# One wire for accumulating transfers in the plan of the order, and a hold for each kind of output product

## The chip, the cores and the metric

The kernel runs on one core of a Trainium2 chip. The metric is the time of the device in microseconds, the median of several executions; less is better. TensorE (PE) multiplies matrices, ScalarE (ACT) and VectorE (DVE) work on elements, GpSimd (POOL) and SyncE (SP) here issue transfers (DMAs). Each engine works through its instructions in the order in which they were written, and waits on semaphores for what the others make.

## What is computed

An attention block over channels and two expert layers, on 6016 tokens of 256 channels, in float32:

```python
def _attn_ref(q, k, v, tau):                  # q, k, v: (1, 6016, 256)
    qn = q / (norm(q, axis=1) + 1e-6); kn = k / (norm(k, axis=1) + 1e-6)
    a = softmax(kn.transpose(0, 2, 1) @ qn / tau)       # 256 x 256
    return v @ a

def _moe_ref(x, w_gate, w_val, w_out, rms_g):  # d_ff = 1536
    xn = x / sqrt(mean(x * x) + 1e-6) * rms_g
    return (silu(xn @ w_gate) * (xn @ w_val)) @ w_out

def _moe2_ref(x, w_in, w_out):                 # d_ff = 2048
    h = x @ w_in
    return (h - tanh(h)) @ w_out

reference = _moe2_ref(_moe_ref(_attn_ref(q, k, v, tau), ...), ...)
```

## The kernel before

**Tiles and stages.** Tokens lie along the free axis, in pairs of blocks of 512; the first pair is short and is worked last, as two blocks of 448. Every float32 product is made of three matmuls in a rounded float32 format: a high and a low part of each operand, and three of the four combinations (`prod`). The attention comes first (up to about 66 us), then the first expert layer, pair by pair, and from about 614 us on the second, in six groups, one for each pair of blocks: `SECOND` is the order 1, 2, 3, 4, 5, 0.

**A unit.** Two by two blocks (of tokens and of hidden channels) are multiplied by a scheme with seven products instead of eight (`unit`). It works in four PSUM banks X, T, Y, Z: X takes A11 B11, T takes S1 T1; ScalarE copies X to Y and T to a tile m5; Y takes S2 T2; VectorE adds Y and m5 to Z; X takes A12 B21 (result c11), Y takes S3 T3 (c22 = Y + m5), Z takes S4 B22 (c12), Y takes A22 T4 (c21). These seven are the main products. For the second layer each result passes through tanh on ScalarE and a subtraction on VectorE. A group has 8 units.

**The output products.** Of the last four units each result is split into high and low parts (`finish_block`; ScalarE makes the high part, VectorE the low one) and multiplied into two of the four accumulators (`Accumulate.push`). For the first four units (`SEVEN2 = 4`) the output too is made with seven products, on sums of the results (`second_seven`, `Seven`): W11 on c11, S1 on c11 + c12, N3 on c12 + c22, M2 on c11 + c12 + c22, and later W12 on c21, S4 on c22, W22 on c11 + c12 + c22 + c21. The sums are made in place by transfers that accumulate, SBUF to SBUF, issued by POOL (`add_by_dma`, line 460): c11 += c12; then c12 += c22 and c11 += c22; then c11 += c21. The second add into c11 must wait until both parts of S1 have been read from it, N3 must wait for one add and M2 for two. After four units `Seven.turn` copies the four accumulators to tiles `part` and combines them by four more adds, each needing the one before; they are used when the group's output leaves. A group so has 20 adds of 256 KB (224 KB in the last group), 120 in all. The split forms live in a ring of four buffers `uh` and `ul` (in the trace uW, uS, uN, uM and uc); each of W11, S1, N3 and M2 of a unit takes the buffer that the same form of the unit before had, and its split waits until that product is done.

**The order.** Nothing is emitted in the order of the loops. `Graph.op` collects each instruction with its engine, an estimate of its cost and the instructions that it must follow. `Graph.run` then plays the engines forward in time and lets each take, of the instructions that are ready, the most urgent; `Graph.latest` goes back from the end and gives each a latest time; six passes of both are made, the one with the earliest planned end is kept, and its order is emitted. For ScalarE, VectorE and the DMA queues, urgency is that latest time. For TensorE it is a key: the main products have the amount of main product work issued before them (`g.main`), and an output product has `g.main` at its birth plus a hold: `LAG0`, `LAG1`, `LAG2` for plain ones (`Accumulate.product`), `LAG7` for the forms (`Seven.form`). The hold is a priority, not a wait: when no instruction with a smaller key is ready, TensorE takes the held one. Transfers of SP are planned on a wire that they share: 1000 ns after issue or behind the one before, then their size at 390 bytes per ns, then 900 ns. An accumulating transfer is planned to occupy POOL for 900 ns and to land 3500 ns after its start (`ADD_LAND`, in `run` line 229 and in `latest` line 286), whatever the one before does. Stores and loads of SP and adds of POOL don't meet in the plan. The waits that the hardware makes are those of the real dependences; the estimates decide only the order.

Of the kernel before, what the change touches and what calls it, by code (L numbers as in the profile page):

```python
# [39 lines left out]
PATIENT, HOLD, TOLERANCE = ("ACT", "DVE"), 900.0, 60.0  # L40
DMA_SETUP, DMA_RATE, DMA_TAIL, DMA_ISSUE = 1000, 390.0, 900, 450
DMA_SLACK = 2200
ADD_ISSUE, ADD_LAND = 900, 3500
STALL, STALL_COST = 40.0, 300.0


# [53 lines left out]
class View:  # L100
# [5 lines left out]
    @property  # L106
    def ap(self):
        return self.f(self.buf.t)
# [14 lines left out]
class Graph:  # L123
# [38 lines left out]
    def run(self):  # L162

        ops = self.ops
        for o in ops:
            o.left, o.ready = len(o.preds), 0.0
        free = dict(READY)
        known = {e: [] for e in free}
        avail = {e: [] for e in free}
        soon = {e: [] for e in free}  # L170
        wire = lag = moved = 0.0

        def rank(o):
            return (o.key if o.eng == "PE" else o.idx if o.late is None else o.late, o.idx)

        def now_known(o):
            if o.eng not in DMAS:
                o.ready += o.slack
            heappush(known[o.eng], (o.ready, o.idx))
            if o.eng not in DMAS:  # L180
                coming(o, o.ready, AHEAD)

        def coming(o, ready, depth):
            for s, data in o.succs:
                if s.left == 1 and s.eng not in DMAS:
                    t = ready + o.cost + self.gap(o, s, data)
                    if s.eng in PATIENT:
                        soon[s.eng].append((t, s.idx))
                    if depth > 1:
                        coming(s, t, depth - 1)  # L190

        for o in ops:
            if not o.left:
                now_known(o)
        order = []
        while len(order) < len(ops):
            best = None
            for e in free:
                if avail[e]:
                    t = free[e]  # L200
                elif known[e]:
                    t = max(free[e], known[e][0][0])
                else:
                    continue
                if best is None or t < best[0]:
                    best = t, e
            t, e = best
            while known[e] and known[e][0][0] <= t:
                o = ops[heappop(known[e])[1]]
                heappush(avail[e], (*rank(o), o))  # L210
            o = heappop(avail[e])[2]
            if e in PATIENT and o.late is not None:
                soon[e] = [x for x in soon[e] if x[0] > t and ops[x[1]].left]
                o = self.patient(o, t, known[e] + soon[e], avail[e], ops, lag)
                if not isinstance(o, Op):
                    free[e] = o
                    continue
            o.start = t
            if e == "PE" and o.late is not None:
                lag = t - o.late  # L220
            if e == "SP":
                free[e] = t + o.cost
                wire = max(t + DMA_SETUP, wire) + o.size / (
                    RAMP_RATE if moved < RAMP_BYTES else DMA_RATE)
                moved += o.size
                o.end = wire + DMA_TAIL + o.slack
            elif e == "POOL":
                free[e] = t + o.cost
                o.end = t + ADD_LAND
            else:  # L230
                stalled = e == "PE" and t > 10 * COLD and t > free[e] + STALL
                o.end = free[e] = t + o.cost * (2 if e == "PE" and t < COLD else 1) + (
                    STALL_COST if stalled else 0.0)
            order.append(o)
            for s, data in o.succs:
                s.left -= 1
                s.ready = max(s.ready, o.end + self.gap(o, s, data))
            for s, _ in o.succs:
                if not s.left:
                    now_known(s)  # L240
        return order
# [28 lines left out]
    def latest(self, order):  # L270

        idle, before, dense = 0.0, None, {}
        for o in order:
            if o.eng == "PE":
                if before is not None:
                    idle += max(0.0, o.start - before)
                dense[o], before = o.start - idle, o.end
        end = max(o.end for o in order) - idle
        for o in reversed(order):
            late = end  # L280
            for s, data in o.succs:
                late = min(late, s.late - self.gap(o, s, data) - (
                    s.slack if s.eng == "PE" else 0.0))
            o.late = late - (
                DMA_SETUP + o.size / DMA_RATE + DMA_TAIL + o.slack if o.eng == "SP" else
                ADD_LAND if o.eng == "POOL" else o.cost)
            if o.eng == "PE":
                o.late = min(o.late, dense[o])

# [27 lines left out]
BEHIND = 4  # L317
WARM = 6
MARGIN = 450.0
LAG0, LAG1, LAG2 = 4100.0, 10000.0, 6500.0  # L320
SWAP7 = False
SEVEN2, LAG7 = 4, 5000.0
SKEW = 2


# [1 line left out]
def attn_moe_kernel(  # L327
# [42 lines left out]
    g = Graph()  # L370
# [92 lines left out]
    def prod(out, w, x, n, start, key=None):  # L463

        (wh, wl), (xh, xl) = w, x

        def emit():
            o = ap(out)
            for i, (a, b) in enumerate(((wh, xh), (wl, xh), (wh, xl))):
                nc.tensor.matmul(  # L470
                    o, ap(a), ap(b), start=start and i == 0, stop=i == 2, skip_group_check=True)

        return g.op("PE", 3 * (n / 2.4 + 13.7), emit, [wh, wl, xh, xl], [out], key=key)
# [813 lines left out]
    class Seven(Accumulate):  # L1287
# [10 lines left out]

        def form(self, j, name, u, t, m):
            first = self.begins(t, m)  # L1300
            prod(self.at(t, m), self.forms[j][name], u, self.sizes[t], first, key=g.main + self.lag7)

        def turn(self):
            n = self.sizes[0]
# [153 lines left out]
    def second_seven(j, x, n, A, keep):  # L1458
# [7 lines left out]
        def out(c):  # L1466
            def f(src):
                t = T[c]
                activation(t, src, AF.Tanh, n)
                tt("sub", t, src, t, n)  # L1470
                if c == "c11":
                    form("W11", "c11", 0, 0)
                if c == "c12":
                    add_by_dma(T["c11"], T["c12"])
                    form("S1", "c11", 1, 0)
                if c == ("c22" if SWAP7 else "c12"):
                    add_by_dma(T["c12"], T["c22"])
                    add_by_dma(T["c11"], T["c22"])
                    form("N3", "c12", 0, 1)
                    form("M2", "c11", 1, 1)  # L1480
                if c == "c21":
                    add_by_dma(T["c11"], T["c21"])
            return f
# [273 lines left out]
```

## Time and profile before

| | |
|---|---|
| median of 3 executions | 1112.81 us (1112.71 to 1113.14) |
| the profiled execution | 1114.58 us, of which 1112.8 from the first to the last instruction |
| TensorE busy | 1099.9 us (99%), 4872 matmuls |
| VectorE, ScalarE busy | 909.7 us (82%), 734.0 us (66%) |
| POOL | 126 instructions, 120 of them adds |
| mean granted clock of TensorE | 0.998 of full |

Times in rows are microseconds from the first instruction unless marked ns. PE is TensorE's matmuls, PEld its weight loads, one for each matmul. A matmul's record is longer than the distance to the next one's start, since they overlap. A tile's name is that of the program without its numbers: `uM` is the high part of form M2, `ulM` the low one, `keepwraw`, `keepvh`, `keepvl`, `keepw12h` hold c11, c22 and c21 of one unit or another, `wc` is c12, `l20h` to `l27h` are the weights of units 0 to 7.

### The profile page before, as it was taken

The numbers are of one execution on the slowest core, as the hardware profiler recorded it, in microseconds if no ns is written. First come the engines' busy times: TensorE is split into PE (matmuls) and PEld (weight loads), VectorE is DVE, ScalarE is ACT, GpSimd is POOL, SyncE is SP. The second block draws the span as 40 slices with busy tenths as digits, with TensorE's granted clock in tenths as the row PEclk, the third lists the DMA queues.
The fourth block names the chain that finished last, engine by engine and source line by source line (L and its number), as shares of the span: only waits on it lengthen the run. The fifth ranks groups of instructions, "written<-read, shape, count | busy, mean of one in ns | idle before, by whom it ended". The sixth has DMA issues, their size and how long they took to land.

```text
span 1112.8 us, 14515 instructions
## 1 busy us (share of the span) xinstructions
PE 1099.9 (99%) x4872; PEld 904.5 (81%) x4872; DVE 909.7 (82%) x1590; ACT 734.0 (66%) x1298; POOL 105.6 (9%) x126
## 2 busy tenths in 40 slices
PE   9999999999999999999999999999999999999998
PEld 8888988888888888888888768778778778878887
DVE  7899897987887888788866878888788888887876
ACT  7675466566566656656656777577587687676674
POOL 0000000000000000000000131130131130230230
PEclk9999999999999999999999999999999999999999
DMA  9952121113212311322322563463463462451451
GB/s 358 380 195 93 58 72 52 45 50 130 68 38 76 90 54 53 114 86 69 127 76 76 131 112 68 93 106 67 95 105 67 99 109 54 102 97 29 105 88 46
DMA packets 61644, 109.44 MB, mean 98 GB/s; under 512 B 7552, under 2 KB 18688, under 8 KB 61568
## 3 DMA queue, kind: packets, MB, share of 16 engines
q1 hardware_dynamic: 43856, 77.32, 20.6%
q0 software_dynamic: 17280, 30.81, 16.2%
q8 instruction: 38, 0.62, 0.2%
q10 hardware_dynamic: 432, 0.38, 0.1%
q14 instruction: 38, 0.31, 0.1%
HBM read 54.79 MB, written 22.83 MB: 70 GB/s over the span
## 4 chain that ended last, share of the span: by engine, by line
PE 70%; issue 11%; DMA 10%; DVE 3%; POOL 3%; ACT 2%; SPq 0%; POOLq 0%; DVEq 0%; ACTq 0%
PE acc L470 27%; PE Yv L470 6%; PE Yg L470 5%; PE Xg L470 4%; PE Xv L470 4%; PE Yh L470 3%; PE S L478 3%; PE v L470 2%; PE g L470 2%; PE Xh L470 2%; PE Zg L470 2%; PE Zv L470 2%; PE Tg L470 2%; PE Tv L470 2%; DMA keepvl<-keepvl 2%
## 5 line engine op out<-in xcount | busy, mean ns | idle before, releaser
L428 ACT ACTIVATE uc<-tc 128x512 fp32r<-128x512 f32 x120 | 74.7, 630 | 93.1 <-DVE tc L443 52.7
L447 DVE TENSOR_TENSOR ulc<-tc,uc 128x512 fp32r<-128x512 f32 x120 | 81.1, 684 | 7.6 <-ACT uc L428 6.9
L460 POOL DMA_DIRECT2D keepwraw<-wc x6 | 5.3, 890 | 767.7 <-DVE ulW L447 767.7
L447 DVE TENSOR_TENSOR ulc<-wc,uc 128x512 fp32r<-128x512 f32 (+1 forms) x96 | 64.5, 678 | 15.0 <-PE acc L470 13.3
L428 ACT ACTIVATE uc<-wc 128x512 fp32r<-128x512 f32 (+1 forms) x96 | 59.8, 623 | 21.4 <-PE acc L470 18.2
L443 DVE TENSOR_TENSOR Zv<-Yv,m5v 128x512 f32<-128x512 f32 x30 | 21.0, 699 | 37.8 <-ACT tc L428 18.2
L478 PE MATMUL S<-q,k 128*128 128x256 f32 x188 | 42.3, 385 | 0.8 <-DMA k<-k_in 0.8
L443 DVE TENSOR_TENSOR Zh<-Yh,m5h 128x512 f32<-128x512 f32 (+1 forms) x48 | 32.9, 685 | 10.2 <-PE Yh L470 6.8
L478 PEld LDWEIGHTS S<-q,k 128*128 128x128 f32 x188 | 35.9, 193 | 5.9 <-DMA q<-q_in 1.1
L428 ACT ACTIVATE wc<-Zh 128x512 f32<-128x512 f32 (+1 forms) x48 | 28.1, 585 | 19.1 <-PE Zh L470 18.4
L443 DVE TENSOR_TENSOR acc<-acc,sq 128x512 f32<-128x512 f32 (+1 forms) x46 | 29.4, 678 | 8.0 <-ACT sq L428 7.3
L428 ACT ACTIVATE m5h<-Th 128x512 f32<-128x512 f32 (+1 forms) x48 | 28.0, 583 | 11.1 <-PE Th L470 11.1
L443 DVE TENSOR_TENSOR wc<-Zh,wc 128x512 f32<-128x512 f32 (+1 forms) x48 | 32.4, 675 | 0.7
L443 DVE TENSOR_TENSOR s<-Yh,m5h 128x512 f32<-128x512 f32 (+1 forms) x48 | 32.3, 673 | 0.7 <-PE Yh L470 0.6
L428 ACT ACTIVATE tc<-Zg 128x512 f32<-128x512 f32 x30 | 17.9, 597 | 22.0 <-PE Zg L470 22.0
L470 PE MATMUL Yh<-T2h,l2s 128*128 128x512 f32 (+1 forms) x96 | 29.7, 390 | 2.4 <-ACT Yh L428 2.4
L428 ACT ACTIVATE tc<-Xg 128x512 f32<-128x512 f32 x30 | 18.0, 599 | 20.9 <-PE Xg L470 20.8
L443 DVE TENSOR_TENSOR tc<-Yg,m5g 128x512 f32<-128x512 f32 x30 | 20.6, 686 | 13.3 <-PE Yg L470 13.3
L428 ACT ACTIVATE Yh<-Xh 128x512 f32<-128x512 f32 (+1 forms) x48 | 27.6, 575 | 5.7 <-DVE wc L443 4.2
L470 PE MATMUL acc<-ulc,w12h 128*128 128x512 f32 x80 | 31.2, 390 | 0.0
L470 PE MATMUL acc<-uc,w11h 128*128 128x512 f32 x80 | 31.2, 389 | 0.0
L470 PE MATMUL acc<-uc,w10h 128*128 128x512 f32 x80 | 31.1, 389 | 0.0
(1094 smaller groups left out, 3849.2 us busy)
## 6 DMA issues: line engine op xcount, KB each, us to landing
vraw<-vT_in SPq DMA_DIRECT2D x11, 512.0 KB, 4.5
y<-r SPq DMA_DIRECT2D x22, 256.0 KB, 2.2
part<-part POOLq DMA_DIRECT2D x20, 256.0 KB, 3.3
outT<-part SPq DMA_DIRECT2D x20, 256.0 KB, 2.2
q<-q_in SPq DMA_DIRECT2D x8, 512.0 KB, 8.4
k<-k_in SPq DMA_DIRECT2D x8, 512.0 KB, 8.4
raw<-w_in_in SPq DMA_DIRECT2D x8, 512.0 KB, 3.9
l<-y SPq DMA_DIRECT2D x16, 256.0 KB, 2.2
```

The costliest lines, as they stand in the source:

```text
L428: nc.scalar.activation(out=ap(out), in_=ap(in_), func=func, **{x: ap(a) for x, a in kw.items()})
L443: return dve(lambda: f(out=ap(out), in0=ap(a), in1=ap(b)), n, 2, [a, b], [out])
L447: lambda: nc.vector.tensor_sub(out=ap(out), in0=ap(in_), in1=f32(ap(hi))), n, 2,
L460: g.op("POOL", ADD_ISSUE, lambda: nc.gpsimd.dma_start(out=ap(out), in_=ap(in_), accum_op=ALU.add), [in_, out], [out])
L470: nc.tensor.matmul(o, ap(a), ap(b), start=start and i == 0, stop=i == 2, skip_group_check=True)
L478: lambda: nc.tensor.matmul(ap(out), ap(a), ap(b), start=start, stop=stop, **kw),
```

## The change

The planned landing of an accumulating transfer changes from 3500 ns after its start to a wire that all of them share: 1850 ns after the start or when the one before has left the wire, 1450 ns on the wire, and 600 ns more. Going back, a POOL step counts 1850 + 1450 + 600 = 3900 ns. The hold of plain output products of the second layer changes from 6500 to 7000 ns of main work, and the one hold of 5000 ns for the forms becomes one for each: W11 4000, S1 and N3 8000, M2 9000, W12, S4 and W22 5000. All instructions are the same; their order on each engine is planned anew.

```diff
-ADD_ISSUE, ADD_LAND = 900, 3500
+ADD_ISSUE, ADD_SETUP, ADD_TIME, ADD_SLACK = 900, 1850, 1450, 600
...
-        wire = lag = moved = 0.0
+        wire = lag = moved = adds = 0.0
...
             elif e == "POOL":
                 free[e] = t + o.cost
-                o.end = t + ADD_LAND
+                adds = max(t + ADD_SETUP, adds) + ADD_TIME
+                o.end = adds + ADD_SLACK
...
-                ADD_LAND if o.eng == "POOL" else o.cost)
+                ADD_SETUP + ADD_TIME + ADD_SLACK if o.eng == "POOL" else o.cost)
...
-LAG0, LAG1, LAG2 = 4100.0, 10000.0, 6500.0
+LAG0, LAG1, LAG2 = 4100.0, 10000.0, 7000.0
 SWAP7 = False
-SEVEN2, LAG7 = 4, 5000.0
+SEVEN2 = 4
+LAG7 = dict(W11=4000., S1=8000., N3=8000., M2=9000., W12=5000., S4=5000., W22=5000.)
...
         def form(self, j, name, u, t, m):
             first = self.begins(t, m)
-            prod(self.at(t, m), self.forms[j][name], u, self.sizes[t], first, key=g.main + self.lag7)
+            prod(self.at(t, m), self.forms[j][name], u, self.sizes[t], first,
+                 key=g.main + self.lag7[name])
```

## Rows read from the trace of the kernel before

**Rows 1.** Stages: stretch, us, busy us (count) by engine, clock, DMA share, GB/s.
```profile
190.00:614.57 424.57, 424.57 (x1866) 348.35 (x1865) 342.21 (x619) 261.18 (x461) 0.00 (x0) 1.00 0.24 78
614.57:694.23 79.66, 77.26 (x326) 59.77 (x324) 65.74 (x105) 58.40 (x105) 17.63 (x20) 1.00 0.50 102
694.23:775.77 81.54, 80.85 (x350) 64.70 (x348) 67.72 (x108) 58.43 (x103) 17.45 (x20) 1.00 0.46 91
775.77:859.85 84.08, 81.99 (x350) 66.00 (x348) 67.88 (x108) 58.62 (x103) 17.45 (x20) 0.98 0.44 88
859.85:941.15 81.30, 80.65 (x350) 64.75 (x348) 67.75 (x108) 58.42 (x103) 17.42 (x20) 1.00 0.46 89
941.15:1023.02 81.87, 81.47 (x349) 64.61 (x348) 67.36 (x108) 57.35 (x102) 17.48 (x20) 1.00 0.41 78
1023.02:1108.40 85.38, 84.89 (x403) 74.80 (x401) 63.93 (x109) 54.42 (x104) 17.48 (x20) 1.00 0.36 67
```

**Rows 2.** Chain that ended last: start, us, what and how many in a row.
```profile
673.99 2.04 PE acc L470 x9
...
1075.23 1.86 PE acc L470 x9
```

**Rows 3.** Order of time: start, us, engine and instruction [idle before, releaser].
```profile
637.83 0.73 PE L470 MATMUL acc<-uM,l2q 128*128 128x512 f32 x2 [0.50 <-ACT uM L428]
...
1071.87 0.47 PE L470 MATMUL Yh<-T3h,l25h 128*128 128x448 f32 x1 [0.38 <-DVE Zh L443]
```

**Rows 4.** Order of time, three adds at the end of a group's fourth unit.
```profile
656.99 0.87 POOL L460 DMA_DIRECT2D keepvl<-keepw12h  x1 [3.58 <-DVE ulM L447]
657.59 1.16 POOL L460 DMA_DIRECT2D wc<-keepw12l  x1
659.00 0.86 POOL L460 DMA_DIRECT2D keepw12h<-keepw12l  x1 [0.25 <-issue]
661.98 0.63 ACT L428 ACTIVATE uN<-wc 128x512 fp32r<-128x512 f32 x1 [0.91 <-DMA wc<-keepw12l]
663.37 0.63 ACT L428 ACTIVATE uM<-keepw12h 128x512 fp32r<-128x512 f32 x1 [0.23 <-DMA keepw12h<-keepw12l]
665.46 0.70 DVE L443 TENSOR_TENSOR Zh<-Yh,m5h 128x512 f32<-128x512 f32 x1
666.21 0.50 PE L470 MATMUL Yh<-T3h,l25h 128*128 128x512 f32 x1 [0.93 <-DVE Zh L443]
```

**Rows 5.** DMA table, 614.57 to 1108.40: queue's share of 16 engines; issues, us to landing.
```profile
q0 software_dynamic: 17280, 30.81, 36.6%
...
part<-part POOLq DMA_DIRECT2D x20, 256.0 KB, 3.3
```

**Rows 6.** SP's order, a chain piece, order of time and stages around 801 us.
```profile
793.31 3.57 SPq L454 DMA_DIRECT2D outT<-part  x4
...
796.32 5.68 DMA keepwraw<-keepwraw
...
802.03 0.63 ACT L428 ACTIVATE uM<-keepwraw 128x512 fp32r<-128x512 f32 x1 [1.50 <-DMA keepwraw<-keepwraw]
803.20 0.73 PE L470 MATMUL Yh<-T2h,l2s 128*128 128x512 f32 x2 [1.81 <-ACT Yh L428]
...
803.20:807.40 4.20, 4.20 (x11) 3.34 (x12) 0.89 (x2) 0.96 (x3) 1.77 (x2) 0.59 0.64 109
```

**Rows 7.** Order of time and a chain piece, fourth group, units 0 to 2.
```profile
870.05 0.62 PE L470 MATMUL Zh<-B22h,l2s 128*128 128x512 f32 x2
...
884.45 3.25 DMA keepvh<-wc
...
885.28 0.69 DVE L447 TENSOR_TENSOR ulM<-keepwraw,uM 128x512 fp32r<-128x512 f32 x1
886.58 0.62 PE L470 MATMUL acc<-uM,l2q 128*128 128x512 f32 x2
...
888.66 0.62 ACT L428 ACTIVATE uS<-keepvh 128x512 fp32r<-128x512 f32 x1
```

**Rows 8.** Waits: engine, line, waited for: us in total, times, longest.
```profile
ACT uW L428 <- PE acc L470: 14.9, 26, 1.4
```

## Prediction

> **What bounds the kernel now.** I read the time by stage first, then the spacing of matmuls, then each place where TensorE falls behind that spacing, followed back to what released it. In the stage table TensorE is busy for all of the 424.57 us before the second expert layer; what is lost is lost in the six groups behind it [rows 1]. The busy column hides part of that, because a matmul's modelled end overlaps the next one's start, so I count matmuls instead. Nine 512-wide matmuls take 2.04 us, 0.2267 us each, nine 448-wide ones 1.86 us, 0.2067 each [rows 2]. A full group has 8 units x 7 main products, 28 products of the group of four and 32 of the other four units: 116 products of 3 matmuls, 348, which is also the count of weight loads in its row. 348 x 0.2267 = 78.89 us. The groups took 81.54, 84.08, 81.30 and 81.87: 2.65 + 5.19 + 2.41 + 2.98 us over that floor. The first has 324 weight loads in 79.66, 6.21 over; the last, 48 matmuls at 0.2267 left over from the group before and 353 448-wide ones at 0.2067, is 1.5 over its 83.85 [rows 1, 2]. Together 21 us, 1.9% of the span: all that a better order can give, since the change adds and removes no instruction.
>
> Next: who took the 21 us? In the six groups 89 intervals between successive matmul starts are more than 0.06 us too long, 19.5 us together. I followed each back: from the matmul to the ScalarE or VectorE instruction that released it, along that engine's queue to the last instruction that had really waited, and to what that one waited for. 82 of them, 18.6 us, end at the landing of an accumulating transfer on POOL's queue; the first and the last are in [rows 3]. The other 0.9 us are seven short waits for VectorE.
>
> [rows 4] is one such place. Three adds are issued at 656.99, 657.59 and 659.00. ScalarE, in order, waits 0.91 us for the second, from 661.98 splits it, and at 663.37 has the third. VectorE's low part, another subtraction and only then Zh follow, and TensorE stands 0.93 us for Zh. Zh has nothing to do with the adds; it stood behind them.
>
> **Why the adds are late.** The plan of before takes 3.5 us from issue to landing, for every add. One alone takes 3.3 us [rows 5], so that is right. But q0's packets fill 36.6% of sixteen engines' time over 493.83 us: 180.7 us for 120 adds, 1.5 us of all engines each [rows 5]. Adds issued closer than that queue up: the second and third of [rows 4] land near 661.96 and 663.35, 4.37 and 4.35 us after issue (0.02 us before the splits that waited for them). I set both formulas against each add's measured issue: 50 of 120 land over 0.05 us later than 3.5 us, 41.1 us in sum. By the new formula (1.85 us, then 1.45 us on one wire shared with the adds before, then 0.6 us) only 12 do, 7.4 us in sum. For the chain of three it gives 3.9, 5.35 and 6.8 us after the first issue; the last two landed at 4.97 and 6.36, so 0.4 us are to spare, where 3.5 us each (4.1 and 5.51) was 0.9 us too early.
>
> **The change part by part.** (1) *One wire for adds, 0.6 us of slack.* No instruction is added; the splits of added forms move back in ScalarE's and VectorE's order, behind work that is ready, and in the second plan constant (the latest times) a POOL step counts 3.9 instead of 3.5 us, so the steps before an add become more urgent by 0.4 us. This removes the places where the landing was late against 3.5 us but not against the new formula: 9.5 of the 18.6 us. I take 85%, 8.1 us, between half (4.8) and all (9.5).
>
> (2) *What the formula doesn't know.* The other 9.1 us hang on adds that landed later than the new formula too, most of them at the head of a group, where SP's stores of the group before run beside them. The worst: four stores are issued on SP from 793.31, the add of 796.32 takes 5.68 us, ScalarE waits 1.50 us in front of a ready Yh copy, TensorE stands 1.81 us, and its granted clock is 0.59 over the next 4.2 us (most of them at the lower level, 1.2 GHz, after TensorE had stood still), 1.7 us lost at that clock [rows 6]: with the late start 3.7 us in one place. The new plan keeps SP's wire and the adds' apart. The lateness of these adds falls from 10.4 to 6.0 us in sum, and (3) takes some of the rest. I take half, 4.5 us, between 0 and 9.1.
>
> (3) *A hold for each kind.* A held product's place is the main product work issued at its birth plus the hold. M2 (two adds deep) is born behind the Z product at 870.05 and runs at 886.58; between lie eleven main products, 11 x 0.68 = 7.5 us of main work, so its hold of 5.0 had run out and it was put where it was expected to be just ready: its low part was done at 885.97 [rows 7]. With 9.0 it runs 1.5 us of main work later; with four held products to seven main ones that is 1.5 x 11/7 = 2.4 us of wall time of margin. N3 and S1 get 3.0 of main work more, W11 1.0 less, which gives its buffer back sooner: ScalarE's uW waits 14.9 us in 26 places for that buffer [rows 8]. The output lag of 7.0 instead of 6.5 us of main work moves 0.8 us of products later. None of it is on a path of its own; its worth is inside (1) and (2). Behind a split that must wait on ScalarE stand the Yh and m5 copies, and TensorE waits for those; that is the price if a hold is too long (third rival).
>
> (4) *A new order's own misses.* Every queue is planned anew, SP's and POOL's too, from the first pass of the planner on. The order of before has 0.9 us of waits without an add in six groups; I charge 1.9 us, between 0 and 4. The tail behind the last matmul stays: the same two halves of one output tile.
>
> The Trainium skill speaks against (1): its page DMA: Bandwidth & Descriptors, in the section on the anatomy of a SWDGE DMA, gives about 2.0 us plus bytes / 436 GB/s, an estimate by that page of 2.6 us for 256 KB with 0.6 us of it on the wire, so that adds issued 0.6 us apart would never queue. By it the new wire would hold splits back for nothing (rival A has the time). Here the trace disagrees: 3.3 us alone, 1.4 to 1.7 us apart in the chain [rows 4, 5].
>
> **Sum.** 8.1 + 4.5 - 1.9 = 10.7 us. The profiled execution took 1114.58 us, 1112.8 of them its span; the median without profile is 1112.81. I take the gain off either: 1103.9 profiled, **1102** as median.
>
> **The rivals.** *A. The stores decide.* The late adds at the head of a group stay as dear as now, with the clock drop, and of (1) only half comes: 4.8 - 1.9 = 2.9, about 1110. For it: the plan has no shared wire of stores and adds. Against: the wait in [rows 6] falls on a copy that was ready, and a split that is planned later stands behind that copy. If adds issued 0.6 us apart landed 0.6 us apart, (1) would be 0 and the sum 4.5 - 1.9 = 2.6 us, 1110 as well; the chain and the 1.5 us of [rows 4, 5] leave that 0.01 of this rival's 0.17. This is what the page's rule above would do.
>
> *B. Nothing.* The waits move to other splits as fast as they are taken away: 1112.8. For it: ScalarE and VectorE run in order, and any estimate that is 1 us short anywhere finds a copy behind it. Against: the 424.57 us before, planned with the same constants but without adds, have no idle time [rows 1].
>
> *C. Slower: the four split buffers.* Each form owns one of four buffers. S1's product moves to 8.0 us of main work, just behind M2's present place: 0.5 us of main work (0.8 of wall time) after 886.58 it would start, near 888.1 end and free the buffer; the next unit's add landed at 887.70 and its split started at 888.66 [rows 7]. From 0.6 us more on ScalarE waits there, with the Yh copy behind it. At a third of the stand in [rows 6], 0.6 us, in each of three units of six groups that is 10.8 us, with its clock drop in half the groups 5.1, against the 9.5 us of (1): 6.4 us slower, 1119. Against it: a hold is only a priority, and the plan lets TensorE take a held product early when no main product is ready.
>
> That the change doesn't reach the order can be left out: the constants enter every planned add.
>
> **How the numbers follow.** Forecast 0.66 (from 1096, all of (1) and (2) less 1.9 us, to 1107, half of (1) and a third of (2) less 1.9), A 0.17, B 0.09, C 0.08. The range from 1096 to 1110.5 takes in A. About 0.2%, 2.2 us, is what a measurement of this kernel can tell from no change: faster 0.83, same 0.09, slower 0.08.
>
> **What would show it.** Right: the four full groups take 79 to 80.5 us; the splits of added forms start without waiting for a landing; chains of three still land near 5.0 and 6.4 us; no stretch of the second layer has a clock under 0.9; M2's products stand 1 us or more behind their low part. Wrong: waits of ScalarE for `acc` in front of uS, uN and uM (C); the same waits for landings at the head of each group beside SP's stores (A); a changed time before 614 us, which I hold at nothing.

## The result, and the profile after

The changed kernel takes 1097.65 us as median (1097.28 to 1098.15), the kernel before 1112.97 beside it: 0.9861 of its time, 95% interval 0.9844 to 0.9878, 15.3 us less. Its profiled execution took 1097.28 us with a span of 1095.5. That of before was 1.6 us longer than its median, so the spans differ by 17.3 us where the medians differ by 15.3.

The stages of the kernel after, cut at the same first matmul of each group as [rows 1] (columns as there):

```profile
190.00:614.30 424.30, 424.30 (x1865) 348.20 (x1864) 341.99 (x619) 261.00 (x460) 0.00 (x0) 1.00 0.25 78
614.30:688.70 74.40, 73.43 (x316) 58.74 (x315) 64.45 (x103) 56.52 (x102) 17.62 (x20) 1.00 0.53 109
688.70:768.72 80.02, 79.91 (x349) 65.09 (x348) 67.41 (x108) 58.40 (x103) 17.53 (x20) 1.00 0.47 93
768.72:848.22 79.50, 79.44 (x349) 65.17 (x348) 67.77 (x108) 58.23 (x103) 17.50 (x20) 1.00 0.47 93
848.22:927.10 78.88, 78.88 (x349) 65.34 (x348) 67.66 (x108) 58.70 (x103) 17.50 (x20) 1.00 0.47 92
927.10:1006.02 78.92, 78.92 (x350) 65.32 (x348) 67.18 (x108) 57.76 (x102) 17.51 (x20) 1.00 0.43 81
1006.02:1091.20 85.18, 85.18 (x412) 76.93 (x410) 64.61 (x111) 55.50 (x107) 17.45 (x20) 1.00 0.36 68
```

Before 614 us next to nothing moved, 0.27 us. The four full groups took 81.54, 84.08, 81.30 and 81.87 us; now they take 80.02, 79.50, 78.88 and 78.92 against a floor of 78.89. Two of them are TensorE without a gap. The first group still is 74.40 - 315 x 0.2267 = 3.0 us over. The clock is at 1.00 in every group.

The end of a fourth unit in the kernel after, in the third group ([rows 4] has that of the first; order of time: start, us, engine and instruction [idle before, releaser]):

```profile
815.76 0.89 POOL L462 DMA_DIRECT2D wc<-keepw12l  x1 [3.72 <-DMA keepw12h<-wc]
816.39 1.16 POOL L462 DMA_DIRECT2D keepvl<-keepw12h  x1
817.43 1.00 POOL L462 DMA_DIRECT2D keepw12h<-keepw12l  x1
819.30 0.63 ACT L430 ACTIVATE uN<-wc 128x512 fp32r<-128x512 f32 x1 [0.20 <-DMA wc<-keepw12l]
...
820.36 0.62 ACT L430 ACTIVATE uW<-keepvraw 128x512 fp32r<-128x512 f32 x1
...
822.92 0.62 ACT L430 ACTIVATE uM<-keepw12h 128x512 fp32r<-128x512 f32 x1
```

The adds are no faster. The second lands 4.88 us and the third 6.41 us after the first issue, where before it was 4.97 and 6.36. But uM's split, which waited 0.23 us for its landing, now comes 0.75 us behind it, with other work before it on ScalarE. Over the second layer the adds keep their price:

```profile
q0 software_dynamic: 17280, 30.81, 37.9%
...
part<-part POOLq DMA_DIRECT2D x20, 256.0 KB, 3.3
```

37.9% of 476.9 us are 180.7 us of all sixteen engines, the very number of [rows 5]; one alone takes the same 3.3 us.

The stores of the third group's head, the place of [rows 6] (SP's issues, a piece of the chain that ended last, then ScalarE and TensorE in order of time):

```profile
788.68 4.71 SPq L456 DMA_DIRECT2D outT<-part  x4
...
792.25 4.90 DMA keepwraw<-keepwraw
...
793.73 0.58 ACT L430 ACTIVATE Yh<-Xh 128x512 f32<-128x512 f32 x1
794.56 0.61 PE L472 MATMUL Yh<-T2h,l2s 128*128 128x512 f32 x2
...
797.17 0.63 ACT L430 ACTIVATE uM<-keepwraw 128x512 fp32r<-128x512 f32 x1 [1.35 <-DMA keepwraw<-keepwraw]
```

The add still takes 4.90 us beside four stores, and ScalarE still waits for it, 1.35 us. But the Yh copy stands 3.4 us ahead of the split instead of behind it, and TensorE's T2 products start without a wait. The 1.81 us and the clock drop of [rows 6] are gone. The largest place that is left is the first group's, beside stores of the first expert layer:

```profile
630.07 2.88 SPq L456 DMA_DIRECT2D y<-r  x3
632.75 0.86 POOL L462 DMA_DIRECT2D keepwraw<-keepwraw  x1 [1.25 <-DVE ulS L449]
638.55 0.63 ACT L430 ACTIVATE uM<-keepwraw 128x512 fp32r<-128x512 f32 x1 [3.27 <-DMA keepwraw<-keepwraw]
639.24 0.73 PE L472 MATMUL acc<-uM,l2q 128*128 128x512 f32 x2 [0.56 <-ACT uM L430]
```

Another is near 741 us, in the second group (POOL's issues, a DMA row for 732 to 736 us with queue and kind, packets, MB and share of 16 engines, and ScalarE):

```profile
730.31 0.87 POOL L462 DMA_DIRECT2D keepw12h<-wc  x1 [0.93 <-DVE keepw12l L445]
736.69 0.86 POOL L462 DMA_DIRECT2D wc<-keepw12l  x1 [5.50 <-DMA keepw12h<-wc]
...
q8 instruction: 1, 0.02, 2.5%
...
740.06 0.63 ACT L430 ACTIVATE uN<-wc 128x512 fp32r<-128x512 f32 x1 [1.32 <-DMA wc<-keepw12l]
```

The first of these adds takes 5.74 us, to 736.05. No transfer of SP is on the way there. What is on the way is one packet of 16 KB on queue q8, whose kind the profile calls instruction; it takes one of the sixteen engines for 1.6 us (2.5% of sixteen engines' 4 us). The second add is issued only behind the first one's landing, and takes 3.35 us itself; ScalarE stands 1.32 us for it and TensorE loses 0.9 us.

### The profile page after: what moved, and what is told of

It reads as the page before. It is cut to its first block, busy times and chain, and to the rows that moved or that the text cites. A ratio compares the mean times of both kernels' runs of the same rounds, so it can differ in the third digit from the quotient of the medians.

```text
span 1095.5 us, 14501 instructions
## 1 busy us (share of the span) xinstructions
PE 1088.7 (99%) x4872; PEld 906.6 (83%) x4872; DVE 908.2 (83%) x1590; ACT 733.6 (67%) x1298; POOL 105.8 (10%) x126
## 3 DMA queue, kind: packets, MB, share of 16 engines
q0 software_dynamic: 17280, 30.81, 16.5%
## 4 chain that ended last, share of the span: by engine, by line
PE 86%; issue 4%; DMA 4%; DVE 2%; ACT 2%; POOL 1%; SPq 0%; DVEq 0%; POOLq 0%; ACTq 0%
PE acc L472 35%; PE Yh L472 7%; PE Yv L472 6%; PE Yg L472 6%; PE Xh L472 4%; PE Xg L472 4%; PE Xv L472 4%; PE S L480 3%; PE v L472 2%; PE g L472 2%; PE Zh L472 2%; PE Th L472 2%; PE Zg L472 2%; PE Zv L472 2%; PE Tg L472 2%
## 5 line engine op out<-in xcount | busy, mean ns | idle before, releaser
L449 DVE TENSOR_TENSOR ulc<-wc,uc 128x512 fp32r<-128x512 f32 (+1 forms) x96 | 64.4, 679 | 12.2 <-ACT uc L430 10.5
L445 DVE TENSOR_TENSOR Zh<-Yh,m5h 128x512 f32<-128x512 f32 (+1 forms) x48 | 32.9, 686 | 18.4 <-PE Yh L472 16.7
L430 ACT ACTIVATE wc<-Zh 128x512 f32<-128x512 f32 (+1 forms) x48 | 28.0, 584 | 21.4 <-PE Zh L472 20.1
L472 PE MATMUL acc<-uc,w12h 128*128 128x512 f32 x80 | 31.2, 389 | 0.0
L472 PE MATMUL acc<-ulc,w11h 128*128 128x512 f32 x80 | 31.1, 389 | 0.0
L472 PE MATMUL acc<-uc,w12l 128*128 128x512 f32 x80 | 31.1, 389 | 0.0
```

The costliest lines, as they stand in the source:

```text
L430: nc.scalar.activation(out=ap(out), in_=ap(in_), func=func, **{x: ap(a) for x, a in kw.items()})
L445: return dve(lambda: f(out=ap(out), in0=ap(a), in1=ap(b)), n, 2, [a, b], [out])
L449: lambda: nc.vector.tensor_sub(out=ap(out), in0=ap(in_), in1=f32(ap(hi))), n, 2,
L472: nc.tensor.matmul(o, ap(a), ap(b), start=start and i == 0, stop=i == 2, skip_group_check=True)
```

## The experiments

Theory 1: TensorE stood behind splits that were planned before their adds had landed; what counts is the planned landing. Theory 2: the holds gave the margin. Theory 1 has two forms: that the plan must know the wire on which adds queue (1a), or that it must only be late enough (1b). For every kernel I took three numbers from its trace, worked out as in the prediction: ScalarE's waits for landings in front of the splits uW, uS, uN and uM (us, times); TensorE's lost time in the first five groups that leads back to a landing (intervals more than 0.06 us over 0.2267, so missed stands under that are not in it); and the ratio of the times with its interval. They stand together here and are used below.

| kernel | median us | ratio, 95% interval | ScalarE's waits for landings | lost to adds, us |
|---|---|---|---|---|
| before | 1112.97 | 1 | 30.8, 45 | 16.5 |
| holds only | 1113.87 | 1.0007, 0.9998 to 1.0016 | 33.4, 43 | 15.2 |
| change, no slack | 1109.98 | 0.9969, 0.9956 to 0.9982 | 36.0, 47 | 12.2 |
| change, W11 9000 | 1107.27 | 0.9954, 0.9937 to 0.9971 | 20.1, 33 | 7.6 |
| change, all holds 9000 | 1107.06 | 0.9946, 0.9932 to 0.9961 | 16.2, 25 | 8.5 |
| 3900 ns flat, holds | 1106.88 | 0.9940, 0.9923 to 0.9956 | 29.4, 41 | 11.4 |
| change, output lag 6500 | 1103.38 | 0.9920, 0.9905 to 0.9935 | 21.9, 24 | 8.0 |
| wire only | 1101.80 | 0.9898, 0.9882 to 0.9915 | 26.4, 35 | 4.7 |
| wire and M2's hold | 1100.56 | 0.9895, 0.9880 to 0.9910 | 24.4, 33 | 4.6 |
| change, SP on the wire | 1098.47 | 0.9864, 0.9849 to 0.9879 | 15.2, 16 | 4.0 |
| **the change** | 1097.65 | 0.9861, 0.9844 to 0.9878 | 15.1, 21 | 3.9 |
| 5000 ns flat, old holds | 1097.17 | 0.9854, 0.9839 to 0.9869 | 9.3, 14 | 0.9 |
| change, slack 1700 | 1095.94 | 0.9854, 0.9839 to 0.9868 | 0, 0 | 0 |
| 5000 ns flat, holds | 1094.60 | 0.9830, 0.9815 to 0.9844 | 1.4, 4 | 0.1 |

The kernel before took 1112.23 to 1113.04 beside them, so ratios are compared, not medians.

Each of these kernels is one order that the planner found, and no run says how far two orders from almost the same constants lie apart. The rows for a later landing run one way in three series (flat with the new holds 3500, 3900, 5000: 1113.87, 1106.88, 1094.60; flat with the old ones 3500, 5000: 1112.97, 1097.17; wire with 0, 600, 1700 ns of slack: 1109.98, 1097.65, 1095.94), so that reading doesn't hang on a single order. The readings of the holds and of the output lag do.

### The wire alone

```diff
-LAG0, LAG1, LAG2 = 4100.0, 10000.0, 7000.0
+LAG0, LAG1, LAG2 = 4100.0, 10000.0, 6500.0
-LAG7 = dict(W11=4000., S1=8000., N3=8000., M2=9000., W12=5000., S4=5000., W22=5000.)
+LAG7 = dict(W11=5000., S1=5000., N3=5000., M2=5000., W12=5000., S4=5000., W22=5000.)
```

> Only the planned landing of an accumulating transfer is changed (one wire, 1850 + 1450 + 600 ns); all holds stay at 5000 and the output lag at 6500. Theory 1 (TensorE stood behind splits whose landing was planned too early): the places where the landing was late against 3.5 us but not against the new formula go, 9.5 us, and some of the 9.1 us beside SP's stores: 1104 us, between 1100 and 1106. Theory 2 (the holds gave the margin, the estimate matters little): 1109 us or more.

Measured: 0.9898, 11.1 us less than before. That is theory 1, and inside its range: the planned landing alone takes what TensorE loses to adds from 16.5 to 4.7 us.

### The holds alone

```diff
-                adds = max(t + ADD_SETUP, adds) + ADD_TIME
-                o.end = adds + ADD_SLACK
+                o.end = t + 3500
...
-                ADD_SETUP + ADD_TIME + ADD_SLACK if o.eng == "POOL" else o.cost)
+                3500 if o.eng == "POOL" else o.cost)
```

> Only the holds are changed (W11 4000, S1 and N3 8000, M2 9000, output lag 7000); every add is still planned to land 3500 ns after its start. Theory 1: the splits of added forms still stand in front of the Yh copies and Zh sums, so only the direct waits of TensorE for uM, uN and uS go, some 3 to 5 us: 1108 to 1110 us. Theory 2: most of the 15 us: 1099 to 1102 us.

Measured: 1.0007. The holds alone bring nothing; theory 2 falls, and the 3 to 5 us that theory 1 gave them here were too many. The same three adds with the holds alone (order of time):

```profile
821.83 0.89 POOL L461 DMA_DIRECT2D wc<-keepw12l  x1 [3.94 <-DVE ulM L448]
822.46 1.15 POOL L461 DMA_DIRECT2D keepvl<-keepw12h  x1
823.04 1.45 POOL L461 DMA_DIRECT2D keepw12h<-keepw12l  x1
825.25 0.63 ACT L429 ACTIVATE uN<-wc 128x512 fp32r<-128x512 f32 x1 [0.73 <-DMA wc<-keepw12l]
...
828.10 0.63 ACT L429 ACTIVATE uM<-keepw12h 128x512 fp32r<-128x512 f32 x1 [0.86 <-DMA keepw12h<-keepw12l]
828.78 0.73 PE L471 MATMUL acc<-uM,l2q 128*128 128x512 f32 x2 [0.28 <-ACT uM L429]
```

M2's hold is 9000 here, and yet its product is the next thing on TensorE when the split is done. The hold didn't put time between them. Over all 24 M2 products the median time from the end of the low part to the product that reads it was 0.19 us before, 0.33 with the holds alone, 0.89 with the wire alone and 1.05 in the change. A hold is a priority: TensorE takes the product early when nothing before it is ready, so its place is set more by when the plan believes it ready. Beside the wire, M2's hold of 9000 instead of 5000 moves it from 0.89 to 1.08 us only. Nor does the time follow this margin: without the slack (below) it is 1.35 us, and TensorE loses 12.2 us.

### One late number instead of a wire

```diff
-ADD_ISSUE, ADD_LAND = 900, 3500
+ADD_ISSUE, ADD_LAND = 900, 5000
```

> The kernel before with one number changed: an add is planned to land 5000 ns after its start, alone or not; no wire, old holds. If any landing planned late enough will do (theory 1 in its plainest form), the time comes near that of the wire alone, within 2 us. If it matters that the plan tells a lone add (3.3 us) from the third of a chain (6.4 us after the first issue), lone adds are used 1.5 us too late, chains of three are right within 0.4 us, and the time stays 2 us or more above the wire alone.

Measured: 0.9854. One number of the kernel before, changed, does as much as the whole change (0.9861) and 4.6 us more than the wire alone, which neither expectation had. A wire isn't needed for it, which speaks against form 1a; the next two runs put that to the test.

The number stands in two places of the planner: a later landing puts the splits later, and in the latest times it makes the steps before an add more urgent. No run changed one without the other. The traces show mostly the first: N3's split starts on average 1.51 us behind the landing of its add instead of 0.27, M2's 0.91 instead of 0.08, while c11 += c12 is issued 3.71 us behind its Z product instead of 3.97. With the new holds as well it is issued after 3.12 us, so the second has some part in the best kernel.

### The wire without its slack, and the slack without the wire

```diff
-ADD_ISSUE, ADD_SETUP, ADD_TIME, ADD_SLACK = 900, 1850, 1450, 600
+ADD_ISSUE, ADD_SETUP, ADD_TIME, ADD_SLACK = 900, 1850, 1450, 0
```

> The change with the 600 ns behind the wire taken away: a lone add is planned to land after 3.3 us, which is what it takes, the second and third of a chain 1.45 us apart. Theory 1a (the shared wire is what counts, the chains were the late ones): within 2 us of the change, 1097 to 1100 us. Theory 1b (what counts is to be planned late, by whatever means): TensorE stalls again where an add meets stores, 1102 us or more.

and, in the change,

```diff
-                adds = max(t + ADD_SETUP, adds) + ADD_TIME
-                o.end = adds + ADD_SLACK
+                o.end = t + 3900
...
-                ADD_SETUP + ADD_TIME + ADD_SLACK if o.eng == "POOL" else o.cost)
+                3900 if o.eng == "POOL" else o.cost)
```

> The change without the wire: every add is planned to land 3900 ns after its start, as a lone one under the change, but the second and third of a chain too; new holds. Theory 1a: chains land 0.5 to 1 us later than planned, as before, and two thirds of the gain are lost: 1107 us or more. Theory 1b: 0.4 us of lateness more than before gives a part of the gain: 1102 to 1107 us.

Measured: 0.9969 without the slack, 0.9940 with 3900 ns flat. The most exact plan of the adds, 3.3 us for one alone and 1.45 us more for each behind it, gives back 12 of the 15 us; 400 ns on a flat number that is wrong for every chain does better. Form 1a falls; 1b holds. The chain does count where the number is tight: at the same 3.9 us for a lone add, the change's wire is 9.2 us ahead of the flat number, and nearly all of the 11.4 us lost with the flat one (all but 0.8) hang on adds that took over 3.55 us. A wire is one way of being late enough for chains, a larger flat number another. Form 1a's number for 3900 ns flat (1107 us or more) was met within 0.2 us, but 1b's range (1102 to 1107) holds it as well, so that run alone doesn't part them. What an exact plan costs is seen where it was exact (order of time, wire without slack):

```profile
819.95 0.89 POOL L462 DMA_DIRECT2D wc<-keepw12l  x1 [3.97 <-DVE s L445]
...
823.37 0.63 ACT L430 ACTIVATE uN<-wc 128x512 fp32r<-128x512 f32 x1 [1.31 <-DMA wc<-keepw12l]
...
826.32 0.70 DVE L445 TENSOR_TENSOR Zh<-Yh,m5h 128x512 f32<-128x512 f32 x1
...
827.07 0.50 PE L472 MATMUL Yh<-T3h,l25h 128*128 128x512 f32 x1 [0.88 <-DVE Zh L445]
```

This add was issued alone and landed just before 823.37, 3.4 us after its issue, 0.1 later than planned. ScalarE had been standing 1.31 us for it. So most of that wait is not in the transfer: its issue came later, against ScalarE's work, than the plan had it. The slack pays for that too. How much of it is the issue and how much ScalarE being early can't be read from a trace, which doesn't have the plan's times. But it is no single case: about 4.9 of the 12.2 us lost without slack lead back to adds that landed within 3.55 us of their issue, and not only, as the expectation had it, to adds beside stores.

### The late number with the new holds

> 5000 ns for every add, no wire, with the new holds. If the holds are worth what they were beside the wire (1101.8 to 1097.65), 1093 to 1095 us, and the best kernel so far. If 5000 ns already leaves hardly any stall on an add (0.9 us in five groups), the holds have nothing left to give: 1096 to 1098 us.

The edit is that of the run with 3900 ns, with 5000. Measured: 0.9830, 1094.60 us, the best kernel here, and better than both the kernel before and the change (its slowest execution took 1094.99, the fastest of the change 1097.28). Its full groups (columns as in [rows 1]):

```profile
686.46:765.39 78.93, 78.93 (x349) 65.34 (x348) 67.69 (x108) 57.76 (x103) 17.44 (x20) 1.00 0.47 94
765.39:844.33 78.94, 78.94 (x350) 65.33 (x348) 67.68 (x108) 57.75 (x103) 17.40 (x20) 1.00 0.47 94
844.33:923.26 78.93, 78.93 (x349) 65.33 (x348) 67.67 (x108) 57.70 (x103) 17.38 (x20) 1.00 0.47 92
923.26:1002.19 78.93, 78.93 (x349) 65.34 (x348) 67.17 (x108) 56.93 (x102) 17.42 (x20) 1.00 0.43 81
```

All four are at the floor of 78.89. The expectation that 0.9 us of stalls leave the holds nothing to give (1096 to 1098) was wrong by 1.4 us; what 5000 flat with the old holds still loses is mostly not behind adds but in short waits for VectorE.

### Later still

```diff
-ADD_ISSUE, ADD_SETUP, ADD_TIME, ADD_SLACK = 900, 1850, 1450, 600
+ADD_ISSUE, ADD_SETUP, ADD_TIME, ADD_SLACK = 900, 1850, 1450, 1700
```

> The change with 1700 instead of 600 ns behind the wire: a lone add is planned to land after 5.0 us, a chain of three up to 7.9 us after its first issue; new holds. If only being late enough counts: as 5000 ns without a wire, 1094 to 1095.5 us. If planning chains later still costs (forms wait for buffers, products bunch): 1096 us or more. If the wire sees what the flat number misses: under 1094 us.

Measured: 0.9854. Not one split waits for a landing, and yet the full groups take 79.2 us each, 0.3 more than 5000 flat; 1.1 us of stands in five groups are now behind ScalarE's copies to `part` at the turn. Being late enough pays; beyond that it costs a little, and the wire brings nothing that 5000 flat lacks.

### SP's transfers on the same wire

```diff
-                adds = max(t + ADD_SETUP, adds) + ADD_TIME
+                adds = wire = max(t + ADD_SETUP, adds, wire) + ADD_TIME
```

> The change, with the adds also planned on the wire of SP's transfers (the next add or transfer starts behind the last of either). The places that are left in the change are adds at the head of a group beside SP's stores and stalls of 4 us in all: if the plan can see them, 1095 to 1097 us; if it places the stores themselves no better, no difference from the change.

Measured: 0.9864, no difference from the change. The first group still loses its time beside the stores (1.4 of the 4.0 us behind the same add as at 638.55).

### One long hold for all forms, and for W11 alone

```diff
-LAG7 = dict(W11=4000., S1=8000., N3=8000., M2=9000., W12=5000., S4=5000., W22=5000.)
+LAG7 = dict(W11=9000., S1=9000., N3=9000., M2=9000., W12=9000., S4=9000., W22=9000.)
```

> The change, but with one hold of 9000 for all seven forms. Each of W11, S1, N3 and M2 owns one of four split buffers, so a long hold of W11 keeps the next unit's W11 split waiting. If each kind needs a hold of its own (rival C of the prediction): ScalarE's waits for acc in front of uW grow from 7.6 us to over 15 us and the time is 1101 us or more. If a hold is only a priority and TensorE takes a held product when it has nothing else: 1097 to 1099 us.

and with W11 alone at 9000:

> The change with W11's hold alone raised from 4000 to 9000; one hold of 9000 for all took 1107.1 us. If W11 is the one whose buffer keeps the next unit's split, and so the reading of c11 and the three adds behind it, waiting: 1103 to 1107 us, with adds of a unit bunched closer. If the loss came from the forms behind the turn (W12, S4, W22) or from S1 and N3: within 2 us of the change.

Measured: 0.9946 and 0.9954. W11's hold alone loses what all of them lose, about 10 us of the 15. A hold too long on a form that owns its buffer is dear, as the prediction's rival C had it for S1, but not by the waits for the buffer. ScalarE's waits for `acc` in the second layer (in the change, with W11 at 9000, with all at 9000: us, times, longest):

```profile
ACT uW L430 <- PE acc L472: 7.6, 17, 1.2
ACT uS L430 <- PE acc L472: 0.2, 1, 0.2
...
ACT uW L430 <- PE acc L472: 7.5, 16, 1.3
...
ACT uW L430 <- PE acc L472: 10.6, 12, 2.1
ACT uS L430 <- PE acc L472: 3.2, 6, 1.4
```

In front of uW they are 7.5 us with W11 at 9000, against 7.6 in the change; with all at 9000, where I expected over 15, they are 10.6. The time is lost again behind landings, 7.6 against 3.9 us, and in 1.6 us for products whose split came just in time. That is most of the 6.3 us that the first five groups take longer than in the change; of the 10.8 us between the two profiled spans, 3.2 are in the last group and 1.3 before the first. In that kernel (order of time, end of a fourth unit):

```profile
817.18 0.63 ACT L430 ACTIVATE uM<-keepvl 128x512 fp32r<-128x512 f32 x1 [0.77 <-DMA keepvl<-keepvl]
...
818.79 0.63 ACT L430 ACTIVATE uS<-keepw12h 128x512 fp32r<-128x512 f32 x1 [0.98 <-DMA keepw12h<-wc]
...
822.73 0.63 ACT L430 ACTIVATE uN<-wc 128x512 fp32r<-128x512 f32 x1 [0.27 <-DMA wc<-keepw12l]
...
826.15 0.63 ACT L430 ACTIVATE uM<-keepw12h 128x512 fp32r<-128x512 f32 x1 [0.29 <-DMA keepw12h<-keepw12l]
...
826.52 0.50 PE L472 MATMUL Yh<-T3h,l25h 128*128 128x512 f32 x1 [0.44 <-DVE Zh L445]
```

four splits wait, 2.3 us together, where the change has two waits at this place, 0.69 us for uM at 813.84 and 0.20 for uN at 819.30. The first add into c11 can't start before W11 has been read from it; that a late W11 split so pushes the three adds behind it is an argument, not shown.

### Which hold

```diff
-LAG7 = dict(W11=4000., S1=8000., N3=8000., M2=9000., W12=5000., S4=5000., W22=5000.)
+LAG7 = dict(W11=5000., S1=5000., N3=5000., M2=9000., W12=5000., S4=5000., W22=5000.)
```

with the output lag at 6500 and the wire as in the change:

> The wire with its 600 ns, output lag 6500, all holds 5000 but M2 at 9000. The prediction's step (3) held that M2, two adds deep, is the form whose product runs the moment it is ready. If M2's margin is what the holds gave beside the wire (1101.8 to 1097.65): 1097.5 to 1099 us. If it was another hold or the output lag: 1101 us or more.

and the change with the output lag alone put back to 6500:

> The change with the output lag of 6500 as before, new wire and new holds of the forms. If the half microsecond of output lag does nothing of its own: 1097 to 1099 us. If it gives room behind the group's turn: 1100 us or more.

Measured: 0.9895, no different from the wire alone (0.9898), and 0.9920. M2's hold is not what gave the last 4 us, though the median of 1100.56 fell between the two expectations. Half a microsecond of output lag is worth 6 us when the forms have the new holds: 8.0 against 3.9 us lost behind adds, and 1.5 us behind other copies. Why is open; two orders that differ by chance are not ruled out. The two edits don't add up (the new holds without the lag are no better than neither), and the output lag alone, with the old holds and the wire, wasn't tried.

## Why the prediction was right, point by point

The forecast was 1102, the range 1096 to 1110.5, the time 1097.65. The direction and the place were right, and so was the cause at TensorE: splits planned before their adds had landed. The gain was 15.3 us where the sum had 10.7, and three reasons on the way were wrong or half right: that the holds give margin, that the late adds are late for SP's stores, and that the plan gains by knowing the chain.

- **Where the time was.** The count against 78.89 us per group, and the tracing of 18.6 us to landings, held: with 5000 flat and new holds those groups reach 78.93, so the floor is a real one, and what had been traced to adds is what went.
- **Step (1), the places late against 3.5 us only.** 8.1 us were taken of 9.5. In the change about 0.5 us is left at such places (near 808 us): 9.0 went.
- **Step (2), the places beside stores.** This term was mis-sized: half of 9.1 us was taken, 4.5. About 2.5 us are left, nearly all in the first group at 638.55 and 647 us, and 0.9 near 741 us behind an add that was on time itself but was issued behind a late one. So 5.7 went, with the clock drop. The lateness of those adds was not the measure. 4.90 us instead of 5.68 is little better, but with the copy planned ahead of the split the same late landing finds nothing behind it. The prediction had this as the argument against its rival A; it should have carried the term. And not all of it was beside stores: about 3 of the 9.1 us, near 647 to 651 and 983 to 986 us in the kernel before, hang on adds with no transfer of SP on the way but a 16 KB packet of q8 on one engine, and so do about 2 of the 3.9 us that are left, at 647 and 741 us. That the packet makes the add late is likely, and no run tested it.
- **Step (3), the holds.** Its reason failed. The 2.4 us of margin for M2 did not come from the hold: alone it gave a median of 0.33 us, the planned landing gave 0.89. That the holds' worth lies inside (1) and (2), as the step said, is borne out by their 0 alone and 4 us beside the wire (2.6 beside 5000 flat).
- **Step (4), misses of the new order.** 1.9 us were charged; the waits without an add fell from 0.9 us to about 0.5 (0.3 of it near 626 us), so the term had the wrong sign. Sum by what was counted: 9.0 + 5.7 + 0.4 = 15.1 us. Both counts are from profiled executions, whose spans differ by 17.3 us; what is missing are stands too short for the count. That 15.1 comes so near to the 15.3 between the medians is chance.
- **The wire.** The prediction took the change's formula for right because it fits the landings (12 of 120 late instead of 50), and so put the gain on knowing the chain. That alone gains little: with the new holds the fit without slack is worth 3.1 us, an error on the late side (5000 flat) 18.4. In the change 11 adds land later than its formula and 57 later than 3.5 us; they are no less late, only expected.
- **The rivals.** A (1110) would have needed the stores' places to stay; their waits on ScalarE did stay (1.35 us at 797.17), which was A's sign, but their price on TensorE went in all groups but the first. B's time is what the holds alone give, and for another reason: there the plan still had 3.5 us. C was about S1's hold of 8000, which the change has, and did not come: ScalarE waits for `acc` once in front of uS, 0.2 us, and not in front of uN and uM. The loss with 9000 for W11 is that of another form.
- **What was to be seen.** Full groups 79 to 80.5 us: 78.88 to 80.02. No clock under 0.9: 1.00. M2's product 1 us behind its low part: 1.05 as median, which shows little, since the kernel without slack has 1.35. Splits that start without waiting for a landing: half right, 15.1 us of such waits are left, of 30.8, but with little behind them that TensorE needs.

## What to carry to other kernels

When a plan written ahead orders engines that work strictly in order, try planning what they wait for later than it is on average, not exactly. Here a step planned too late was covered by other ready work, at 0.3 us a group where it was far too late; one planned too early stopped all that was queued behind it on its engine, and the cost showed on another engine, under another name. So trace each stand of the bounding engine back along the queue of its releaser until something has really waited, and try one pessimistic number before a better model.

## What the runs showed of the hardware

An accumulating transfer of 256 KB takes 3.3 us alone in all these orders, and the mean over the 120 stays between 3.68 and 3.84 us; beside SP's transfers (4.90 and 5.68 us in the places shown) or behind other adds single ones take up to 6.8 us. The order moved their price on TensorE from 16.5 us to 0.1 without moving their mean by more than 0.12 us.

What makes single adds later than the wire's formula is not stores alone. In the kernel before and the change together, one of the 154 adds that have neither a transfer of SP nor a q8 packet on the way is more than 0.05 us later than the formula, 9 of the 44 with a transfer of SP alone, 9 of the 34 with a q8 packet alone, and 4 of the 8 with both. These packets are 16 KB, each takes one of the sixteen engines for 0.9 to 1.6 us, and 17 of them come in the second layer of either kernel.

The Trainium skill's page DMA: Bandwidth & Descriptors, in its section on the anatomy of a SWDGE DMA, would make an add of 256 KB about 2.6 us, an estimate by that page; for these accumulating transfers the traces disagree, and a plan by that number would be 0.7 us early even for a lone add.

I had spaced 448-wide matmuls at 0.2067 us. In the change's last group 85.18 us less 63 x 0.2267 for the 512-wide ones left over leave 70.9 us for 347 of them, 0.2043 each: the 1.5 us that I had the last group over its floor were rather 2.4.
